# Start-up loads, stacked tails and 128-row turns in a fused attention, gated-MLP and Fourier-mixing kernel

## The chip, the core and the metric

The kernel runs on one core of a Trainium2 chip. The metric is the device time of one execution in microseconds; the median of three executions is given. One further execution was taken by the hardware profiler, and every row shown here is from it. The names in the rows: PE is TensorE's matmul stream and PEld its weight loads, DVE is VectorE, ACT is ScalarE, POOL is GpSimd, SP is SyncE; a name with a q at its end is that engine's DMA queue.

## What is computed

Attention with a soft cap on the scores, a gated MLP with a spatial projection, and a mixing layer with cosine and sine, one behind the other. Four batches, 12 heads, 448 positions, 64 numbers per head, 768 model columns.

```python
def _attn_ref(q, k, v, cap):                     # q, k, v: (4, 12, 448, 64)
    scores = np.matmul(q, k.transpose(0, 1, 3, 2)) / np.sqrt(64)
    scores = cap * np.tanh(scores / cap)
    attn = np.exp(scores - np.max(scores, axis=-1, keepdims=True))
    return np.matmul(attn / (np.sum(attn, axis=-1, keepdims=True) + 1e-09), v)

def _moe_ref(x, w_in, w_spatial, b_spatial, w_out):   # x: (4, 448, 768), w_in: (768, 1024)
    h = np.maximum(x @ w_in, 0.0)
    u, v = h[..., :512], h[..., 512:]
    v_n = (v - mean(v)) / np.sqrt(var(v) + 1e-06)
    v_s = np.einsum('ts,bsd->btd', w_spatial, v_n) + b_spatial[None, :, None]
    return (u * v_s) @ w_out

def _moe2_ref(x, w_theta, w_tok_r, w_tok_i, w_ch):
    theta = x @ w_theta
    y = einsum('ts,bsd->btd', w_tok_r, x * cos(theta)) + einsum('ts,bsd->btd', w_tok_i, x * sin(theta))
    u = x + y
    return u + np.maximum(u @ w_ch, 0.0)
```

## The kernel before

**Order of the work.** The program is written as small operations (`op(engine, due, cost, function, r=..., w=...)`) with the slots and tiles that each reads and writes. A list of numbers, `ORDER`, sorts all of them into one sequence, and every engine carries out its own part of that sequence strictly in order. An operation that waits holds back all that stands behind it on its engine, DMA issues included: loads are issued by SP, ACT or POOL in the place that the list gives them.

**Stages by time.** Heads go in pairs. The first six pairs of batch 0 are done in plain f32 ("direct"; 0 to about 80 us); the later ones as products of a high and a low part in a shorter format, with the first MLP's matmuls between them (to about 355 us). The last batch's MLP, the next layer's angles `th_ps`, the turning of `w_tok` and the mixing `y_ps` follow (to about 650 us), and then the product with `w_ch`.

**The start.** PE runs 11 matmuls on zeros (`idle`), then turns pair 0's q and k (`tqk`): rows 0 to 383 of each head from `rq` and `rk`, the last 64 rows from `tt`. Seven more `idle` matmuls follow, then the scores `sc`. A pair's scores come in groups: group 0 multiplies the last 64 keys of both heads at once, through a block-diagonal tile `bd` that DVE and ACT fill from the turned keys in PSUM. Group 1 and the others use the copy `qk`. Pair 0's loads are issued by SP and ACT, in 256-byte packets. The weights `w_in` come as 8-byte words (`w_in_bits`, 512 KB a load, 12 loads, the first six on POOL's queue) and are turned into floats by POOL (L442), DVE (L448 to L463) and POOL (L1032, L402); at most three such tiles are held at first.

**Tails of 64.** 448 positions are three blocks of 128 and one of 64. In `moe1_v` (the half of the first MLP's hidden layer that is normalised) batches 0 to 2 have their tails' high and low parts stacked as 128 columns (`beside`, tile `x_tail`). The last batch does three 64-column products instead for each of the six blocks of model columns. Turns of `w_spatial` (`w_sp_ps`) and `w_tok` (`tok_ps`) go in four matmuls against an identity each, the fourth with 64 rows.

Of the kernel before, what the change touches and what calls it, by code (L numbers as in the profile page):

```python
# [10 lines left out]
F32 = mybir.dt.float32  # L11
# [327 lines left out]
def attn_moe_moe2_kernel(ctx: ExitStack, tc: tile.TileContext, q, k, v, cap, w_in, w_sp, b_sp, w_out,  # L339
# [9 lines left out]
    SK = 4  # L349
# [147 lines left out]
    XQ = ("pool", "sp")  # L497
    HE = ("act", "act")
    LE = ("dve","dve")
    xhl = {}  # L500

    v1 = [att.tile([128, NC + 1, 2, D], F32, tag="vhl", name="v1", bufs=2) for _ in range(2)]

# [17 lines left out]
    def split_out(b, p, t):  # L521
# [4 lines left out]
        def hi():  # L526
            st["x"] = keep.tile([128, 2, S], F32R, tag="x%d" % p, name="x")
            for n, x in enumerate("hl"):
                xhl[x, b, p] = st["x"][:, n, :]
# [1804 lines left out]
```

## Time and profile before

| | |
|---|---|
| median of 3 executions | 757.33 us (756.39 to 757.44) |
| profiled execution, its own time | 756.88 us |
| its span (first to last instruction) | 755.1 us |
| PE busy | 740.6 us, 98% of the span |
| DVE, ACT, POOL busy | 601.2, 471.2, 327.6 us |

The time of an execution is that of the span plus what lies around it: here 756.88 - 755.1 = 1.8 us. Busy time is the time in which an engine had an instruction at work; what is left is idle, and a row's bracket gives the idle time just before it with the work that ended it.

### The profile page before, as it was taken

The numbers are of one execution on the slowest core, as the hardware profiler recorded it, in microseconds if no ns is written. First come the engines' busy times: TensorE is split into PE (matmuls) and PEld (weight loads), VectorE is DVE, ScalarE is ACT, GpSimd is POOL, SyncE is SP. The second block draws the span as 40 slices with busy tenths as digits, with TensorE's granted clock in tenths as the row PEclk, the third lists the DMA queues.
The fourth block names the chain that finished last, engine by engine and source line by source line (L and its number), as shares of the span: only waits on it lengthen the run. The fifth ranks groups of instructions, "written<-read, shape, count | busy, mean of one in ns | idle before, by whom it ended". The sixth has DMA issues, their size and how long they took to land.

```text
span 755.1 us, 11422 instructions
## 1 busy us (share of the span) xinstructions
PE 740.6 (98%) x3951; PEld 631.2 (84%) x3951; DVE 601.2 (80%) x979; ACT 471.2 (62%) x792; POOL 327.6 (43%) x419
## 2 busy tenths in 40 slices
PE   7999999999999999999999999999999999999997
PEld 3444678988889888988899999999989999998997
DVE  2567987888878986999987577888778887999955
ACT  2889787888788878896554545453423532554553
POOL 3537677553655465462100001332222234688570
PEclk9999999999999999999999999999999999999999
DMA  5766233242442441332243330002210000000145
GB/s 149 201 162 181 64 101 84 77 108 51 116 96 46 108 112 40 94 79 67 84 149 103 102 112 22 1 22 64 62 44 22 22 1 1 0 1 1 38 109 148
DMA packets 82718, 57.47 MB, mean 76 GB/s; under 512 B 50338, under 2 KB 75908, under 8 KB 82660
## 3 DMA queue, kind: packets, MB, share of 16 engines
q1 hardware_dynamic: 80580, 52.94, 26.9%
q0 software_dynamic: 1056, 3.54, 1.4%
q8 instruction: 31, 0.51, 0.3%
q10 hardware_dynamic: 1024, 0.26, 0.2%
q14 instruction: 27, 0.22, 0.1%
HBM read 43.72 MB, written 5.62 MB: 65 GB/s over the span
## 4 chain that ended last, share of the span: by engine, by line
PE 85%; DVE 5%; ACT 3%; DMA 3%; POOL 1%; issue 1%; SPq 0%; DVEq 0%; ACTq 0%; POOLq 0%
PE ps_mm L399 20%; PE y_ps L399 13%; PE acc L399 12%; PE th_ps L399 12%; PE f_ps L399 9%; PE sc L399 8%; PE ps_sum L399 3%; PE ps_av L399 3%; PE tqk L691 2%; PE o_ps L2155 1%; DMA w_in_bits<-in_moe_w_in_dram 1%; PE x_ps L1605 1%; ACT e L808 1%; DMA y<-y 1%; DMA rq<-in_q_dram 1%
## 5 line engine op out<-in xcount | busy, mean ns | idle before, releaser
L399 PE MATMUL y_ps<-tok_h,zt 128*128 128x448 f32 x312 | 98.5, 368 | 0.0
L805 ACT ACTIVATE e<-sc,icap 128x896 f32<-128x896 f32 x72 | 72.1, 1007 | 5.9 <-PE sc L399 5.3
L808 ACT ACTIVATE e<-e,cap_sb 128x896 f32<-128x896 f32 x72 | 74.5, 1043 | 0.6
L402 DVE TENSOR_TENSOR ll<-e,hh 128x896 fp32r<-128x896 f32 x54 | 61.2, 1136 | 8.7 <-ACT hh L813 5.6
L399 PEld LDWEIGHTS y_ps<-tok_h,zt 128*128 128x128 f32 x312 | 58.8, 188 | 4.5
L399 PE MATMUL th_ps<-th_ah,x 128*128 128x256 f32 x288 | 58.0, 285 | 0.0
L399 PE MATMUL y_ps<-tok_l,zt 128*128 128x448 f32 x156 | 57.4, 368 | 0.0
L402 POOL TENSOR_TENSOR zt<-z,zt 128x1024 fp32r<-128x1024 f32 x12 | 28.9, 2407 | 63.1 <-ACT zt L1720 63.1
L1659 POOL TENSOR_SCALAR n<-n 128x512 f32<-128x512 f32 (+1 forms) x24 | 15.8, 663 | 82.2 <-DVE n L1656 82.2
L399 PE MATMUL f_ps<-x,S 128*128 128x448 f32 x216 | 48.4, 371 | 0.3 <-POOL x L402 0.3
L399 PE MATMUL ps_mm<-x,w_in_h 128*128 128x448 f32 x168 | 48.5, 370 | 0.0
L399 PE MATMUL ps_mm<-w_in_h,x 128*128 128x512 f32 (+1 forms) x132 | 46.8, 398 | 1.2 <-DVE w_sp_l L402 1.2
L399 PEld LDWEIGHTS th_ps<-th_ah,x 128*128 128x128 f32 x288 | 47.1, 190 | 0.8
L402 POOL TENSOR_TENSOR x<-x,x 128x384 fp32r<-128x384 f32 (+1 forms) x15 | 18.5, 1239 | 66.7 <-ACT x L1546 58.4
L399 PEld LDWEIGHTS f_ps<-x,S 128*128 128x128 f32 x216 | 39.9, 188 | 3.9 <-POOL x L402 0.6
L1720 ACT CAST zt<-z 128x1024 fp32r<-128x1024 f32 (+2 forms) x36 | 24.3, 691 | 29.1 <-DVE z L1691 23.1
L895 DVE COPY s<-acc 1x448 f32<-1x448 f32 (+1 forms) x48 | 29.7, 618 | 14.0 <-ACT xun L887 6.6
L399 PE MATMUL th_ps<-th_al,x 128*128 128x256 f32 x144 | 40.7, 282 | 0.0
L399 PE MATMUL acc<-ll,vh 128*128 128x448 f32 x108 | 39.7, 368 | 0.8 <-DVE ll L402 0.8
L399 PE MATMUL acc<-hh,vh 128*128 128x448 f32 x108 | 39.6, 367 | 0.0
L399 PE MATMUL sc<-yl,XH 128*128 128x448 f32 x108 | 39.5, 366 | 0.0
L399 PE MATMUL acc<-hh,vl 128*64 128x448 f32 x108 | 39.4, 364 | 0.0
(323 smaller groups left out, 2293.9 us busy)
## 6 DMA issues: line engine op xcount, KB each, us to landing
y<-y SPq DMA_DIRECT2D x54, 112.0 KB, 2.2
bits<-in_moe_w_ch_dram SPq DMA_DIRECT2D x12, 384.0 KB, 3.1
out_dram<-o SPq DMA_DIRECT2D x23, 192.0 KB, 2.4
rq<-in_q_dram SPq DMA_DIRECT2D x33, 128.0 KB, 2.8
r<-d SPq DMA_DIRECT2D x16, 224.0 KB, 3.7
rk<-in_k_dram SPq DMA_DIRECT2D x9, 384.0 KB, 3.7
rv<-in_v_dram SPq DMA_DIRECT2D x18, 192.0 KB, 2.6
w_in_bits<-in_moe_w_in_dram POOLq DMA_DIRECT2D x6, 512.0 KB, 5.4
```

Of the source, the lines that this page charges most:

```text
L399: nc.tensor.matmul(out=ps, lhsT=a, rhs=r, start=(first and i == 0), stop=(last and i == len(terms) - 1))
L402: (engine or nc.vector).tensor_tensor(out=o, in0=x, in1=f32(hi), op=ALU.subtract)
L691: nc.tensor.transpose(o, a, ident)
L805: nc.scalar.activation(out=st["e", g], in_=src, func=ACTF.Tanh, scale=icap)
L808: nc.scalar.activation(out=st["e", g], in_=st["e", g], func=ACTF.Exp, scale=cap_sb)
L895: nc.vector.tensor_copy(out=st["s"][64 * hd:64 * hd + n, :], in_=st["acc", hd][64 - x0:64 - x0 + n, :])
L1605: nc.tensor.transpose(o, x2(b, m)[:, p * 128:p * 128 + 128], ident)
L1659: nc.gpsimd.tensor_scalar(out=sd["n"], in0=sd["n"], scalar1=1.0, scalar2=-MAGIC, op0=ALU.mult, op1=ALU.add)
L1720: nc.scalar.copy(out=o, in_=a)
L2155: nc.tensor.transpose(st["t"][0:w, i * 128:(i + 1) * 128], x2(b, m)[:, i * 128:i * 128 + w], ident)
```

## The change

It has five parts. (1) The tail of pair 0's keys is loaded through POOL's queue instead of ACT's. (2) `bd` is filled by POOL from `qk` in SBUF, for all six direct pairs, instead of by DVE and ACT from PSUM; the first `w_in` loads read the mark `begun`, which POOL's second copy of pair 0 now sets, so they stand behind it. In direct pairs group 1 is scored ahead of group 0. (3) The last batch's tails are stacked too: POOL copies them into a tile `x_tail`, which sits in the slot of the next layer's tile `x2_2` until that is opened, later than before. (4) Turns of `w_tok` and `w_spatial` take 128 rows in the fourth block, whose lower half POOL clears. (5) `ORDER` is a new list.

```diff
-            QT = ("sp", "act") if p == 0 else ("sp", "sp")
+            QT = ("sp", "pool") if p == 0 else ("sp", "sp")
...
             def block(hd):
-                copy = nc.scalar.copy if hd else nc.vector.tensor_copy
-                copy(out=bd[HD[hd], p % 2, 64 * hd:64 * hd + 64], in_=st["k"][HD[hd], 0:64])
+                nc.gpsimd.tensor_copy(out=bd[HD[hd], p % 2, 64 * hd:64 * hd + 64], in_=st["qk"][HD[hd], 1, 0:64])
-            op("act", t0 - FR - 5.2, ca, lambda: plain(0), r=ks, w=[kqk] + ["begun"] * (b == p == 0), banks=ks[:1])
+            op("act", t0 - FR - 5.2, ca, lambda: plain(0), r=ks, w=[kqk], banks=ks[:1])
...
-                op(("dve", "act")[hd], t0 - FR - 4.9, 0.2, lambda hd=hd: block(hd), r=ks, w=[(kb, hd)], banks=ks[1:])
+                op("pool", t0 - FR - 4.2, 0.25, lambda hd=hd: block(hd), r=[kqk, (kqk, 1)],
+                   w=[(kb, hd)] + ["begun"] * (b == p == hd - 1 == 0), port=True)
...
+        if direct:
+            steps[:2] = [(1, 0.0, 4, 0.8, 2.3, 3.25, 3.8), (0, 1.4, 3, 1.9, 3.2, 3.85, 4.15)]
...
+            if j == 3:
+                nc.gpsimd.memset(st["p"][UP, 3, :], 0.0)
...
-                nc.tensor.transpose(st[i][0:m, j * 128:j * 128 + n], st["p"][0:n, j, i * 128:i * 128 + m],
-                                    ident[0:n, 0:n])
+                nc.tensor.transpose(st[i][0:m, j * 128:j * 128 + 128], st["p"][:, j, i * 128:i * 128 + m], ident)
...
-        beside = i == SK - 1 and b < B - 1
+        beside = i == SK - 1
+        kx = "xt" if b < B - 1 else "xu"
+        if beside and b == B - 1:
+            def tail(j):
+                if "x" not in x_last:
+                    x_last["x"] = pools["xs"].tile([128, NP, 2, 64], F32R, tag="x2_%d" % (B - 2), name="x_tail")
+                x = f32(xpair[b, j])
+                nc.gpsimd.tensor_scalar(out=x_last["x"][:, j], in0=x[:, :, 384:448], scalar1=1.0, scalar2=0.0,
+                                        op0=ALU.mult, op1=ALU.add)
...
-                        products(ps, [(xt_[:, j].rearrange("p a n -> p (a n)"), wi["h", 1, j])], first, last)
+                        x = xt_ if b < B - 1 else x_last["x"]
+                        products(ps, [(x[:, j].rearrange("p a n -> p (a n)"), wi["h", 1, j])], first, last)
...
+        def pad():
+            ta[1] = gpool.tile([128, 2, 2 * S], F32, tag="g", name="ta")
+            nc.gpsimd.memset(ta[1][UP, 1, :], 0.0)
...
-                a, o = ta[j // 2][0:n, j % 2], st["ps"][:, j * 128:j * 128 + n]
+                a, o = ta[j // 2][:, j % 2], st["ps"][:, j * 128:j * 128 + 128]
                 if kk < NC:
-                    nc.tensor.transpose(o, a[:, kk * 128:(kk + 1) * 128], ident[0:n, 0:n])
+                    nc.tensor.transpose(o, a[:, kk * 128:(kk + 1) * 128], ident)
...
+    op("none", u - 1.0, 0.0, lambda: open_x2(B - 2), w=[("x2", B - 2, m) for m in range(KD)] + ["x_last"]
+       + [("xu" + x, j) for x in "hl" for j in range(KD)])
```

Three places show how instructions move. The first is POOL's list from the first instruction behind the start barrier; `v_103` and `v_104` are two tiles of values whose columns of ones and zeros POOL sets. Before:

```order
masks.py:197 MEMSET ident 128x128
L1019 DMA w_in_bits<-in_moe_w_in_dram 128x512
masks.py:199 ISA
masks.py:199 AFFINE_SELECT ident<-ident 128x128
L1019 DMA w_in_bits<-in_moe_w_in_dram 128x512
L505 MEMSET v_103 128x3x64
L506 MEMSET v_103 128x3x64
L507 MEMSET v_103 128x256
L508 MEMSET v_103 64x64
L509 MEMSET v_103 64x64
L442 TENSOR_SCALAR w_in_bits<-w_in_bits 128x512 x2
L1019 DMA w_in_bits<-in_moe_w_in_dram 128x512
```

The same place in the changed kernel:

```order
L511 MEMSET v_103 64x64
L512 MEMSET v_103 64x64
L615 DMA tt<-in_k_dram 64x2x64
L748 COPY bd<-qk 64x64 x2
L1026 DMA w_in_bits<-in_moe_w_in_dram 128x512 x2
L508 MEMSET v_104 128x3x64
L509 MEMSET v_104 128x3x64
L510 MEMSET v_104 128x256
L511 MEMSET v_104 64x64
L512 MEMSET v_104 64x64
L1026 DMA w_in_bits<-in_moe_w_in_dram 128x512
L748 COPY bd<-qk 64x64
```

Ahead of these rows the changed list has only the identity and the other `v_103` settings, so the first two `w_in` loads, which were the second and the fifth row, now stand behind the load of the keys' tail and behind two copies that need pair 0's turned keys.

The second place is PE's list in the last batch's `moe1_v`, at the first of its 64-column products; `ps_sum` belongs to the other half of the hidden layer. Before:

```order
L399 MATMUL ps_mm<-w_in_h,x 64x512
L399 MATMUL ps_mm<-w_in_l,x 64x512
L399 MATMUL ps_mm<-w_in_h,x 64x512 x2
L399 MATMUL ps_mm<-w_in_l,x 64x512
L399 MATMUL ps_mm<-w_in_h,x 64x512 x2
L399 MATMUL ps_mm<-w_in_l,x 64x512
L399 MATMUL ps_mm<-w_in_h,x 64x512
L399 MATMUL ps_sum<-w_in_h,x 128x512
```

The same place in the changed kernel:

```order
L400 MATMUL ps_mm<-w_in_h,x_tail 128x512
L400 MATMUL ps_mm<-w_in_l,x 64x512 x2
L400 MATMUL ps_mm<-w_in_h,x_tail 128x512
L400 MATMUL ps_mm<-w_in_l,x 64x512
L400 MATMUL ps_mm<-w_in_h,x_tail 128x512
L400 MATMUL ps_mm<-w_in_l,x 64x512
L400 MATMUL ps_mm<-w_in_h,x_tail 128x512
L400 MATMUL ps_mm<-w_in_l,x 64x512
L400 MATMUL ps_mm<-w_in_h,x_tail 128x512
L400 MATMUL ps_sum<-w_in_h,x 128x512
```

For each block of model columns two 64-column products with `w_in_h` became one with 128 columns; over the whole tail 18 matmuls became 12.

The third place is PE's list at the first turn of `w_tok`, between two products of the angles. Before:

```order
L399 MATMUL th_ps<-th_ah,x 128x256
L1481 MATMUL tok_ps<-ident,ta 128x128 x3
L1481 MATMUL tok_ps<-ident,ta 128x64
L1481 MATMUL tok_ps<-ident,ta 128x128 x3
L1481 MATMUL tok_ps<-ident,ta 128x64
L399 MATMUL th_ps<-th_ah,x 128x256
```

The same place in the changed kernel:

```order
L400 MATMUL th_ps<-th_ah,x 128x256
L1509 MATMUL tok_ps<-ident,ta 128x128 x8
L400 MATMUL th_ps<-th_ah,x 128x256
```

Each turn of 64 rows became one of 128, in the same place; there are nine such among the turns of `w_tok` and four among those of `w_spatial`.

## Rows read from the trace of the kernel before

**Rows 1.** The page: its span and the engines' busy time.
```profile
span 755.1 us, 11422 instructions
PE 740.6 (98%) x3951; PEld 631.2 (84%) x3951; DVE 601.2 (80%) x979; ACT 471.2 (62%) x792; POOL 327.6 (43%) x419
```

**Rows 2.** Windows: stretch, length, busy us of each engine, granted clock, DMA share, GB/s.
```profile
20.00:60.00 40.00, 40.00 (x145) 17.00 (x144) 24.93 (x42) 34.21 (x50) 20.14 (x23) 1.00 0.69 190
60.00:70.00 10.00, 9.63 (x33) 3.78 (x33) 5.63 (x10) 9.93 (x15) 7.17 (x10) 1.00 0.64 164
80.00:90.00 10.00, 8.32 (x39) 6.21 (x38) 9.88 (x13) 7.45 (x11) 3.99 (x6) 1.00 0.13 39
90.00:100.00 10.00, 9.17 (x45) 6.98 (x44) 9.14 (x9) 7.76 (x12) 6.81 (x9) 1.00 0.34 82
350.00:450.00 100.00, 100.00 (x488) 89.77 (x487) 80.95 (x160) 51.62 (x105) 8.70 (x11) 1.00 0.35 105
```

**Rows 3.** Timeline of PE, 0 to 20 us: start, us, engine, line, operation, [idle before].
```profile
1.18 4.88 PE L515 MATMUL idle<-zero 128*128 128x512 bf16 x11 [1.18 <-DVE zero L374]
9.75 0.87 PE L677 MATMUL tqk<-ident,rq 128*128 128x128 f32 x3 [3.70 <-DMA tt<-in_k_dram]
11.55 2.82 PE L515 MATMUL idle<-zero 128*128 128x512 bf16 x7
16.00 0.55 PE L677 MATMUL tqk<-ident,rq 128*128 128x128 f32 x3
19.30 1.02 PE L399 MATMUL sc<-qk,bd 128*128 128x448 f32 x2 [0.35 <-ACT e L805]
```

**Rows 4.** Timeline of SP and POOL, the start: issues, a setting, the first conversion.
```profile
1.29 0.74 POOL L1019 DMA_DIRECT2D w_in_bits<-in_moe_w_in_dram  x1 [0.36 <-issue]
1.55 1.45 SPq L601 DMA_DIRECT2D rq<-in_q_dram  x2
3.36 0.33 POOL L507 MEMSET v<- 128x256 f32 x1
7.20 0.64 POOL L442 TENSOR_SCALAR w_in_bits<-w_in_bits 128x512 f32<-128x512 f32 x1 [3.10 <-DMA w_in_bits<-in_moe_w_in_dram]
```

**Rows 5.** DMA packets by queue, 3.0 to 4.5 us, then 8.0 to 9.0 us.
```profile
q0 software_dynamic: 87, 0.34, 80.7%
q10 hardware_dynamic: 45, 0.01, 3.4%
...
q1 hardware_dynamic: 1004, 0.23, 113.8%
```

**Rows 6.** Timeline of DVE and POOL: first conversion of `w_in`, its fourth load, `w_sp_p`.
```profile
17.42 0.41 DVE L448 TENSOR_SCALAR w_in_f<-w_in_bits 128x512 uint32<-128x512 uint32 x1
20.54 0.58 POOL L1019 DMA_DIRECT2D w_in_bits<-in_moe_w_in_dram  x1
69.48 2.76 POOL L1070 TENSOR_SCALAR w_sp_p<-w_sp_n 128x384 f32<-128x384 f32 x6
```

**Rows 7.** Timeline of PE: turns of `w_spatial`, the last batch's tail, turns of `w_tok`, of `x`.
```profile
72.60 1.43 PE L1077 MATMUL w_sp_ps<-ident,w_sp_p 128*128 128x128 f32 x8
73.96 1.77 PE L399 MATMUL acc<-e,v 128*128 128x448 f32 x4
...
363.92 0.39 PE L399 MATMUL ps_mm<-w_in_l,x 128*64 128x512 f32 x1
364.15 0.61 PE L399 MATMUL ps_mm<-w_in_h,x 128*64 128x512 f32 x2
...
454.18 1.37 PE L1481 MATMUL tok_ps<-ident,ta 128*128 128x128 f32 x8
455.49 0.38 PE L399 MATMUL th_ps<-th_ah,x 128*128 128x256 f32 x1
...
466.96 0.82 PE L1605 MATMUL x_ps<-ident,x 128*128 128x128 f32 x6
467.62 0.27 PE L1607 MATMUL x_ps<-ident,x 128*128 128x128 f32 x1
```

More of the change, by code (lines that the diff above doesn't have):

```diff
@@ L500, in attn_moe_moe2_kernel @@
     xhl = {}
+    xpair = {}
+    x_last = {}
     v1 = [att.tile([128, NC + 1, 2, D], F32, tag="vhl", name="v1", bufs=2) for _ in range(2)]
@@ L529, in hi @@
                 xhl[x, b, p] = st["x"][:, n, :]
+            xpair[b, p] = st["x"]
             if HE[b > 0] == "act":
@@ L909, in attention @@
         K = {}
-        for g, ts, n, tt, te, th, tl in ((0, 0.0, 3, 0.65, 2.3, 2.95, 3.25), (1, 0.6, 4, 1.4, 2.9, 3.85, 4.4),
-                                         (2, 2.6, 4, 3.8, 4.7, 5.95, 6.5), (3, 4.8, 4, 5.7, 6.6, 7.8, 8.7)):
+        steps = [(0, 0.0, 3, 0.65, 2.3, 2.95, 3.25), (1, 0.6, 4, 1.4, 2.9, 3.85, 4.4),
+                 (2, 2.6, 4, 3.8, 4.7, 5.95, 6.5), (3, 4.8, 4, 5.7, 6.6, 7.8, 8.7)]
+        if direct:
+            steps[:2] = [(1, 0.0, 4, 0.8, 2.3, 3.25, 3.8), (0, 1.4, 3, 1.9, 3.2, 3.85, 4.15)]
+        for g, ts, n, tt, te, th, tl in steps:
             ks = ring("s", 2)
@@ L1075, in transposes @@
             for j in range(SK):
-                n = 128 if j < 3 else 64
-                nc.tensor.transpose(st[i][0:m, j * 128:j * 128 + n], st["p"][0:n, j, i * 128:i * 128 + m],
-                                    ident[0:n, 0:n])
+                nc.tensor.transpose(st[i][0:m, j * 128:j * 128 + 128], st["p"][:, j, i * 128:i * 128 + m], ident)
         def hi(i):
@@ L1154, in relu @@
             nc.scalar.activation(out=st["v"], in_=st["ps"][0:n, 0:HF], func=ACTF.Relu)
-        beside = i == SK - 1 and b < B - 1
+        beside = i == SK - 1
[7 more added lines that the diff above has]
+                                        op0=ALU.mult, op1=ALU.add)
+            for j in range(KD):
+                op("pool", due - 4.0 + 0.3 * j, 0.3, lambda j=j: tail(j), r=[("xh", j), ("xl", j), "region"],
+                   w=[("xuh", j), ("xul", j)] + (["x_last"] if j == 0 else []), port=True)
         def step(j, ps, first, last):
@@ L1193, in moe1_v @@
             (0.43 if beside else 0.65, j,
-             [("w", x, 1, j) for x in "hl"] + [("xh", j), ("xl", j)] + [("xt" + x, j) for x in "hl"] * beside)
+             [("w", x, 1, j) for x in "hl"] + [("xh", j), ("xl", j)] + [(kx + x, j) for x in "hl"] * beside)
             for j in range(KD)], span, early, lambda ps, j, first, last: step(j, ps, first, last))
@@ L1298, in close_attention @@
             wo[x] = pools["w15"].tile([128, KF, DM], F32R, name="w_out_" + x)
-        for b in range(B - 1):
-            x2_tiles[b] = pools["xs"].tile([128, KD, S], F32, name="x2_%d" % b)
+        for b in range(B - 2):
+            open_x2(b)
     p15 = ExitStack()
@@ L1304, in attn_moe_moe2_kernel, with open_x2 @@
     x2_tiles = {}
+    def open_x2(b):
+        x2_tiles[b] = pools["xs"].tile([128, KD, S], F32, name="x2_%d" % b)
     def x2(b, m):
@@ L1432, in load_tok @@
         slots = [ring("g", 3), ring("g", 3)]
+        def pad():
+            ta[1] = gpool.tile([128, 2, 2 * S], F32, tag="g", name="ta")
+            nc.gpsimd.memset(ta[1][UP, 1, :], 0.0)
+        op("pool", t - 1.0, 0.5, pad, r=["region"], w=[slots[1]])
         for j in range(SK):
@@ L1477, in transposes @@
             for j in range(SK):
-                n = 128 if j < 3 else 64
-                a, o = ta[j // 2][0:n, j % 2], st["ps"][:, j * 128:j * 128 + n]
+                a, o = ta[j // 2][:, j % 2], st["ps"][:, j * 128:j * 128 + 128]
                 if kk < NC:
-                    nc.tensor.transpose(o, a[:, kk * 128:(kk + 1) * 128], ident[0:n, 0:n])
+                    nc.tensor.transpose(o, a[:, kk * 128:(kk + 1) * 128], ident)
                     continue
-                nc.tensor.transpose(o, a[:, S - 128:S], ident[0:n, 0:n])
-                nc.tensor.transpose(o[LO], a[:, S:S + 64], ident[0:n, 0:n])
+                nc.tensor.transpose(o, a[:, S - 128:S], ident)
+                nc.tensor.transpose(o[LO], a[:, S:S + 64], ident)
         def dst(x):
```

335 rows, old and new, of the table ORDER are left out of this document.

## The prediction

> **What bounds the kernel now.** I read the page first: PE is busy 740.6 of 755.1 us [rows 1], so nothing can gain much unless it shortens PE's work or fills one of its 14.5 us of pauses. The windows show where these are. The last batch's MLP has none, PE 100.00 of 100 us [rows 2]. From 80 to 100 us PE has 8.32 and 9.17 of 10, and there DVE has 9.88 and 9.14: 2.5 us of pauses in a stretch that DVE sets, with an ACT at 9.93 of 10 just ahead of it (60 to 70). PE's timeline of the first 20 us shows the largest pause: its zero matmuls end at 6.06, its first turn starts at 9.75 [rows 3]. That is 3.7 us, a quarter of all.
>
> **The start.** The bracket of that pause names a load of key tails, but the instruction waits on the two loads of pair 0's queries (issued 1.55, [rows 4]) and on the identity. SP has issued both by 1.55 + 1.45 = 3.0 us; what is late is the data. POOL issues `w_in` at 1.29, and in 3.0 to 4.5 us its queue q0 holds 80.7% of the DMA time with 87 packets, while q1, the queries' queue, has no row at all and q10, ACT's, moves 45 packets [rows 5]. With `w_in` nearly gone, q1 moves 1004 packets in the one microsecond from 8.0. Pair 0's q and k are 1792 packets (four loads of 384 and two of 128): at that rate 1.8 us. If they flow from 3.0 us, when SP has issued both query loads, they are there at 4.8 us, and with a few hundred packets of pair 1 mixed in at 5.3. The key tail goes through POOL behind five settings of at most 0.33 us each [rows 4] and the identity; I estimate its issue at 2.7 us and the landing of its 128 packets under 6. All that is before the zero matmuls end at 6.06. So the first turn moves from 9.75 to about 6.1: **3.6 us**. If packets still get in each other's way by a microsecond, 2.7.
>
> A rule weighed against that: the Trainium skill, DMA: Bandwidth & Descriptors, Queues, rings and completion order, says that each DMA engine goes round the queues that have work, a packet at a time. By that rule the queries should have had every second turn beside `w_in`, and the loads would be slow by themselves. The row with no q1 packet does not agree. By the rule the start would gain a microsecond instead of 3.6, which is rival B.
>
> **The clock in the start.** The granted clock reads 1.00 in every stretch, but spacings say more: eleven 512-column zeros take 4.88 us, so about 0.43 each, which is the lower level (1.2 GHz); late in the kernel 512 columns take 0.23 (363.92 to 364.15, [rows 7]). Three turns take 0.87 us at 9.75 and 0.55 at 16.00 [rows 3]. So PE reached its upper level only after the turns, having worked on without a break from 9.75. In the changed kernel it works on from 1.18 with no pause at 6.06. If the upper level comes as late behind the turns as now, nothing is gained; if it is there when the turns begin, the seven zeros take 7 x 0.23 = 1.6 instead of 2.8 us and the six large turns 2 x 0.32 less: 1.8 us. I take **1.2**, nearer the upper end, since by 6.1 us PE will have worked unbroken longer than it had before the present rise; the earlier 4.88 us did not raise it, so I don't take all.
>
> **What now stands behind POOL's copies.** `bd` needs DVE's `qk` copy first and then two POOL copies; group 1 goes first, so PE asks for `bd` only after one group of scores and pair 1's turns, over 2 us later. Hidden. ACT loses its six copies, and with group 1 first the 0.35 us pause at 19.30 should go: **0.35** (0 to 0.35).
>
> The first `w_in` load moves from 1.29 to about 9.5 us. Before, it landed for POOL at 7.20 and DVE touched it at 17.42 [rows 4, 6]: ten microseconds to spare. Landing some 5.9 us after its issue, as now, gives 15.4, where DVE, moved up by 4.8 to 5.2 us with PE, would want it at about 12.4. The chain starts 3 us late against PE. The fourth load waits for a freed tile (20.54), not for the first load; DVE is busy only 24.93 of 40 us from 20 to 60 [rows 2], so I let the chain catch up, at nothing. If it does not, see rival C.
>
> **Stacked tail.** The 64-column products have the spacing of whole ones, 0.23 us (363.92 to 364.15), [rows 7]; 18 become 12: 6 x 0.23 = **1.4 us** on a PE without pauses. POOL's six copies lie beside (POOL 8.70 of 100 us there, [rows 2]), as do the three added operations of ACT and DVE.
>
> A rule that speaks against it: the Trainium skill, TensorEngine Tiling (Array Packing), Tiling Modes, has 128-by-64 tiles that work independently of each other. By it, pairs of 64-column products side by side would cost half, and stacking would gain nothing, which is rival E. The spacing shows no such overlap here: by the row the term is 1.4, by the rule 0.
>
> **Turns by 128 rows.** Eight turns with two of 64 rows take 454.18 to 455.49 = 1.31 us; turns of 128 rows alone have a spacing of 0.66 / 6 = 0.11 (466.96 to 467.62), [rows 7]. Eight of them, the last followed closely, take about 0.80. So 0.26 us per 64-row turn: three blocks of eight give 1.5, the block of four 0.26, the last block, with its two at the end, 0.2. Sum **2.0 us**, PE having no pause there. POOL's clearing of the padding lies long before.
>
> For `w_spatial` the first block of eight takes 72.60 to 73.96, 1.36 us, so 0.5 could be saved there and 0.55 in the other two. But all of it lies ahead of or inside the stretch that DVE sets, and DVE's list there is the same: **0** (at most 1.05).
>
> **Sum.** 3.6 + 1.2 + 0.35 + 1.4 + 2.0 = 8.55 us. The profiled execution took 756.88, so 748.3; it lies 0.45 below the median of the three, so I give **748.5 us**. The forecast's own range: starts of 2.7 to 3.7, clock 0 to 1.8, pauses 0 to 0.35, tail 1.4, turns 1.9 to 2.1, `w_spatial` 0 to 1.05: 6.0 to 10.4 gained, or 746.7 to 751.1.
>
> **Rivals.**
>
> B. The queries are slow by themselves: their 256-byte packets, not `w_in`, set the 9.75. For it: q10's packets come slowly too, and with 8.0 to 9.0 us full the rate is bound by packets. Against it: the empty q1. The start then gains about 1 and the clock nothing: 1.0 + 0.35 + 1.4 + 2.0 = 4.75, so 752.6.
>
> C. The start's gain is lost again at 60 to 100 us. ACT and then DVE set the pace there, and what feeds them is also the `w_in` chain. If that stays 3 us late against PE, then PE pauses longer before its turns of `w_spatial`, whose source `w_sp_p` POOL finishes at 69.48 + 2.76 = 72.24 [rows 6], 0.36 before PE takes it. Of its 3 us some 0.4 are PE's to spare there, and 2.6 of the 8.55 go: 751.1.
>
> D. Slower. The whole `w_in` chain hangs on its first load and moves with it. That load lands at 15.4 instead of 7.2, 8.2 us later; `w_sp_p` would be done at 80.4, where PE arrives at 72.6 - 5.15 = 67.4: a stall of 13 us, against gains of 8.55, so 757.3 + 4.4 = 761.7. It decides from the point at which the chain is late by more than the 8.55 gained plus the 0.36 to spare, less the 5.15 that PE comes early: 3.8 us later than now at 72 us. Against it: the ten microseconds for which the first tile lay unused, and a fourth load that waits for the conversion.
>
> E. The 64-column products lie side by side already, and stacking gains nothing: 748.5 + 1.4 = 749.9. Against it: their spacing of 0.23 us, that of whole ones.
>
> **Chances.** Forecast 0.68, B 0.11, C 0.11, D 0.04, E 0.03, other mishaps 0.03. A measurement of this kernel tells 0.2%, 1.5 us, from no change. Faster by more than that are the forecast, B, C and E: 0.93; the same 0.03; slower 0.04. The range takes in B's and C's times and the forecast's lower end: 746.3 to 752.6.
>
> **What would show it.** PE's first turn at about 6.1 and no pause ahead of it; first scores at about 9.5; zeros between them under 2.8 us; `w_in` issues behind the `bd` copies, at 9 to 10; no q0 rows before them but the tail's; no pause of PE that POOL's `bd` ends; 12 matmuls in the last batch's tail at 0.23; blocks of eight turns at 0.8. The prediction is wrong if the first turn starts after 7, if PE's pauses from 80 to 100 us grow by more than 1 us over 2.5, or if waits for `x_tail` or `x2_2` appear where PE had none.

## The result, and the profile after

The changed kernel takes **749.46 us** (median of 4 executions, 748.24 to 750.56); the kernel before, beside it on the same chip, 756.86 us (756.06 to 757.44). The ratio is 0.9903, with a 95% interval of 0.9881 to 0.9924: 7.4 us, or 1.0%, faster. 748.5 us was forecast. The profiled execution took 750.56 us, one of the slower two of the four; a second profile of the same kernel took 748.49 (it is the run `after_again` below).

The page of the changed kernel, its span and busy times, answers to [rows 1]:

```profile
span 748.8 us, 11416 instructions
PE 735.2 (98%) x3945; PEld 629.0 (84%) x3945; DVE 606.3 (81%) x974; ACT 471.6 (63%) x787; POOL 335.1 (45%) x440
```

PE's work fell by 5.4 us and its pauses from 14.5 to 13.6. With the start's pause of 3.7 filled, 10.8 should have been left: so 2.8 us more of them came elsewhere than went. The windows of the changed kernel, beside [rows 2], show where:

```profile
20.00:60.00 40.00, 39.83 (x148) 16.97 (x147) 29.62 (x40) 35.49 (x50) 25.62 (x33) 1.00 0.76 202
70.00:80.00 10.00, 7.74 (x34) 5.12 (x33) 9.80 (x15) 7.61 (x15) 5.97 (x11) 1.00 0.26 72
80.00:90.00 10.00, 9.16 (x44) 7.00 (x43) 9.20 (x9) 7.01 (x10) 5.49 (x7) 1.00 0.33 88
90.00:100.00 10.00, 10.00 (x47) 7.95 (x46) 7.89 (x12) 7.31 (x11) 7.34 (x12) 1.00 0.52 135
350.00:450.00 100.00, 99.64 (x494) 89.55 (x493) 81.03 (x162) 51.61 (x105) 11.59 (x18) 1.00 0.34 105
```

The program stands some 6 us further on in the same window, so the stretch that DVE fills now lies at 70 to 80 us, and PE has 2.3 us of pauses in it. What was not there before is in the last row: PE pauses by 0.36 us in the last batch's MLP, where it had none.

PE's timeline from 0 to 20 us, beside [rows 3]:

```profile
1.18 4.87 PE L518 MATMUL idle<-zero 128*128 128x512 bf16 x11 [1.18 <-DVE zero L375]
5.85 0.85 PE L681 MATMUL tqk<-ident,rq 128*128 128x128 f32 x3
7.22 1.67 PE L518 MATMUL idle<-zero 128*128 128x512 bf16 x7
8.82 1.02 PE L400 MATMUL sc<-qk 64*128 64x448 f32 x4
18.45 0.92 PE L400 MATMUL sc<-qk,bd 128*128 128x448 f32 x2
```

The first turn starts at 5.85 without a bracket: there is no pause ahead of it. The seven zeros take 1.67 us in place of 2.82, and the first score starts at 8.82. In the kernel before that was at 14.20:

```profile
14.20 0.92 PE L399 MATMUL sc<-qk,bd 128*128 128x448 f32 x2
```

No product that needs `bd` has a bracket. The timeline of SP, POOL and DVE in the same stretch, beside [rows 4, 6]:

```profile
0.73 1.58 SPq L605 DMA_DIRECT2D rq<-in_q_dram  x2
...
2.25 0.80 POOL L615 DMA_DIRECT2D tt<-in_k_dram  x1
8.12 0.50 POOL L748 COPY bd<-qk 64x64 f32<-64x64 f32 x2 [5.06 <-DVE qk L745]
8.56 1.15 POOL L1026 DMA_DIRECT2D w_in_bits<-in_moe_w_in_dram  x2
...
13.11 0.43 DVE L449 TENSOR_SCALAR w_in_f<-w_in_bits 128x512 uint32<-128x512 uint32 x1 [1.44 <-DMA w_in_bits<-in_moe_w_in_dram]
```

SP issues the two loads of pair 0's queries at 0.73, in [rows 4] at 1.55: the new list moved them too. `w_in` is issued at 8.56, behind the two copies into `bd`, and DVE now waits 1.44 us for it; in [rows 6] it had lain ready for ten. The DMA packets by queue from 3.0 to 4.5 us, the window of [rows 5]:

```profile
q1 hardware_dynamic: 576, 0.14, 41.5%
q10 hardware_dynamic: 361, 0.09, 26.2%
q0 software_dynamic: 29, 0.03, 6.8%
```

q1, which had no packet there, moves 576. PE's timeline at the last batch's tail and at the first turn of `w_tok`, beside [rows 7]:

```profile
365.13 0.40 PE L400 MATMUL ps_mm<-w_in_h,x_tail 128*128 128x512 f32 x1
365.88 0.48 PE L400 MATMUL ps_sum<-gh,w_out_h 128*128 128x448 f32 x1 [0.36 <-ACT vt L1161]
...
449.81 1.03 PE L1509 MATMUL tok_ps<-ident,ta 128*128 128x128 f32 x8
450.60 0.36 PE L400 MATMUL th_ps<-th_ah,x 128*128 128x256 f32 x1
```

Eight turns take 0.79 us (449.81 to 450.60) in place of 1.31. At the end of the stacked tail PE waits for ACT, where the kernel before went on.

### The profile page after: what moved, and what is told of

Read it like the earlier page. It is cut to its first block, busy times and chain, and to the rows that moved or that the text cites. A ratio compares the mean times of both kernels' runs of the same rounds, so it can differ in the third digit from the quotient of the medians.

```text
span 748.8 us, 11416 instructions
## 1 busy us (share of the span) xinstructions
PE 735.2 (98%) x3945; PEld 629.0 (84%) x3945; DVE 606.3 (81%) x974; ACT 471.6 (63%) x787; POOL 335.1 (45%) x440
## 4 chain that ended last, share of the span: by engine, by line
PE 78%; DVE 13%; ACT 3%; POOL 2%; issue 2%; DMA 1%; SPq 0%; DVEq 0%; ACTq 0%; POOLq 0%
PE ps_mm L400 17%; PE y_ps L400 12%; PE th_ps L400 11%; PE acc L400 10%; PE f_ps L400 8%; PE sc L400 8%; PE ps_sum L400 3%; PE ps_av L400 3%; PE tqk L695 2%; DVE x L403 1%; PE o_ps L2185 1%; DVE ll L403 1%; DVE s L983 1%; PE x_ps L1635 1%; DVE xun L986 1%
## 5 line engine op out<-in xcount | busy, mean ns | idle before, releaser
L403 POOL TENSOR_TENSOR zt<-z,zt 128x1024 fp32r<-128x1024 f32 x12 | 30.4, 2533 | 66.8 <-ACT zt L1750 66.8
L400 PE MATMUL ps_mm<-w_in_h,x 128*128 128x512 f32 x120 | 43.1, 398 | 3.1 <-DVE w_sp_l L403 1.7
L1707 ACT ACTIVATE z<-z 128x512 f32<-128x512 f32 (+1 forms) x24 | 12.5, 523 | 41.6 <-DVE z L1701 41.4
```

What stands on the lines that cost most here:

```text
L400: nc.tensor.matmul(out=ps, lhsT=a, rhs=r, start=(first and i == 0), stop=(last and i == len(terms) - 1))
L403: (engine or nc.vector).tensor_tensor(out=o, in0=x, in1=f32(hi), op=ALU.subtract)
L1707: nc.scalar.activation(out=z[:, 0:n_], in_=r[:, 0:n_], func=ACTF.Sin)
```

## The experiments

Each was run with executions of the kernel before on the same chip, and the ratio is to those. "a" in a name is the changed kernel with an edit, "b" the kernel before with one.

| run | median, us | ratio to before, 95% interval |
|---|---|---|
| the changed kernel | 749.46 | 0.9903 [0.9881, 0.9924] |
| after_again | 749.38 | 0.9892 [0.9876, 0.9908] |
| a_win_first | 755.92 | 0.9976 [0.9961, 0.9991] |
| a_zeros5 | 751.58 | 0.9927 [0.9908, 0.9946] |
| b_start | 755.80 | 0.9980 [0.9966, 0.9993] |
| b_parts | 754.59 | 0.9958 [0.9941, 0.9975] |
| b_fix | 753.42 | 0.9953 [0.9934, 0.9971] |
| a_tok64 | 751.53 | 0.9928 [0.9914, 0.9942] |
| a_sp64 | 749.72 | 0.9896 [0.9881, 0.9911] |
| a_tail64 | 750.18 | 0.9902 [0.9888, 0.9916] |
| a_cast | 751.07 | 0.9914 [0.9896, 0.9932] |
| a_order | 748.51 | 0.9880 [0.9859, 0.9900] |
| a_both | 747.24 | 0.9869 [0.9851, 0.9888] |

Differences of a microsecond between medians are within what executions of one kernel differ by; for such the profiles are set side by side, from one landmark in the program to the next.

### The changed kernel a second time

> The changed kernel once more, for a second profile. Its four executions so far lie in two pairs, 748.2 and 748.6, 750.3 and 750.6, and the profile at hand is of the upper pair. Theory: the upper pair is made by a load of reciprocals (r<-d) that lands late at 318.8 us, after which VectorE works without a gap to 345 us and TensorE pauses 0.92 and 1.37 us; then a profile of a lower execution shows that load landing 1 us or more sooner and less than 1 us of these two pauses. Rival: the upper pair has the clock's upper level later in the start; then the first score stands after 9.5 us in one pair and at 8.8 in the other. Time expected: 749.4, from 748 to 751.

749.38 us; its span is 746.7, 2.1 shorter than that of the profile above. The first score is at 8.93, so the start is not what differs. The pauses differ: at 74, 77, 319 and 505 us the slower execution has 0.4 to 0.6 us more each. The theory holds for one of its two pauses: that at 319 goes from 0.92 to 0.37, that at 342 is 1.37 in both. Where two profiles are compared below, this one stands for the changed kernel.

### The start: whose loads come first

The first two `w_in` loads go back to the head of POOL's list:

```diff
+for i in (44, 30):
+    ORDER.remove(i)
+    ORDER.insert(0, i)
...
-        op("pool" if pool else "sp", t - 9.0, 1.05 if pool else 0.53, load, w=[kb], r=["begun"], lag=4.0, early=0.0)
+        op("pool" if pool else "sp", t - 9.0, 1.05 if pool else 0.53, load, w=[kb], r=["begun"] * (half == 0 or kk not in (0, 2)), lag=4.0, early=0.0)
```

> The changed kernel with the first two loads of w_in back at the head of GpSimd's list; nothing else differs. Theory (the loads of w_in hold the 256-byte packets back): the first turn goes from 5.85 back to 9 to 10 us, the upper clock level comes only after the turns, the first score stands at 13 to 14.3 instead of 8.8 us, and the time rises by 4 to 5.5 us to 753.5 to 755. Rival (the new order of the q and k loads, queries first, is what helped): first turn at 5.9 to 7, time within 1.5 us of 749.5.

755.92 us, 6.5 more than the changed kernel and a microsecond over the upper end of the expectation. PE's timeline of this run, up to 14 us:

```profile
1.18 4.16 PE L522 MATMUL idle<-zero 128*128 128x512 bf16 x11 [1.18 <-DVE zero L379]
6.87 0.52 PE L685 MATMUL tqk<-ident,rq 128*128 128x128 f32 x3 [1.52 <-DMA rq<-in_q_dram]
8.81 0.37 PE L687 MATMUL tqk<-ident,tt 64*128 64x64 f32 x1 [1.43 <-DMA tt<-in_q_dram]
10.36 3.19 PE L522 MATMUL idle<-zero 128*128 128x512 bf16 x7
13.48 1.12 PE L404 MATMUL sc<-qk 64*128 64x448 f32 x2
```

With `w_in` ahead the queries' loads are late again (two pauses, 2.95 us), the zeros between are back at 3.19 us for seven, and the first score comes 4.6 us later. The order of the issues on POOL does this: all other edits of the start are still in. The other 1.9 us are behind the first score, where profiles of the changed list differ by as much (337.4 to 340.0 us from the first score to the last `acc`, 339.3 here). The first turn, at 6.87 and not at 9 to 10, is earlier than the theory had it: with SP's query loads issued at 0.73 the first two come sooner, as the rival has it, but the turns of the tails then wait.

### The clock: zeros left out

```diff
-    warm_up(11, -9.0, [])
+    warm_up(5, -9.0, [])
```

Six of the first matmuls on zeros are left out; the output does not depend on them.

> The changed kernel (749.4, first turn 5.85, first score 8.8 us) with 5 zero matmuls ahead of the first turn instead of 11, so TensorE pauses from 3.3 us until the loads have landed. It shows when they land: theory, between 5.0 and 5.85 us. Theory of the clock (the upper level came at 6.3 us because TensorE had worked without a break from 1.2): with the break the turns and most of the seven zeros behind them run at the lower level, first score at 9.5 to 11 us, time 0.7 to 2 us up. Rival (the level comes at its own time, break or not): first score at 8.2 to 8.9 us, time within 0.6 us of 749.4.

751.58 us, 2.2 longer. PE's timeline of this run:

```profile
5.03 0.88 PE L681 MATMUL tqk<-ident,rq 128*128 128x128 f32 x3 [1.54 <-DMA rq<-in_q_dram]
6.83 3.19 PE L518 MATMUL idle<-zero 128*128 128x512 bf16 x7
9.95 1.73 PE L400 MATMUL sc<-qk 64*128 64x448 f32 x4
```

This run shows two things. The queries are there at 5.03 us, so the changed kernel's first turn, at 5.85, comes 0.8 us later than they allow. And PE, which paused for 1.54 us, turns 0.8 earlier but runs its seven zeros in 3.19 / 7 = 0.46 us each (the lower level, 1.2 GHz) where the changed kernel, with no pause, runs them in 1.67 / 7 = 0.24 (the upper, 2.4 GHz); the four scores take 1.73 us, not 1.02. At the first score the changed list with all zeros is ahead by 1.0 us (8.93 in `after_again`); the rest of the 2.2 comes later, where profiles of one list differ by as much. The granted clock reads 1.00 in these stretches all the same.

`a_zeros5` has both a pause and fewer matmuls. `a_win_first`, with all eleven zeros, tells them apart: its eleven take 4.16 us in place of 4.87, since the last are spaced 0.22 (the upper level), the three turns at 6.87 take 0.52, and behind the second pause the seven zeros take 3.19. Here the granted clock shows the fall too; its window from 9 to 12 us, with the clock third from the end:

```profile
9.00:12.00 3.00, 2.81 (x9) 1.42 (x9) 0.94 (x3) 0.53 (x1) 0.61 (x3) 0.50 0.59 106
```

The column has 0.95 from 7 to 8 us and 0.50 from 8 to 9: the level that PE had reached was lost in the second pause. Work without a break from 1.18 us gives the upper level before the seven zeros, and that is worth more than turning 0.8 us earlier.

### What the new order list is for

First the start alone (parts 1 and 2 of the change) on the kernel before, with the old list; then all parts of the code with the old list, in which the operations that are new were put in by hand. The renumbered lists are left out of the cut.

```diff
-            QT = ("sp", "act") if p == 0 else ("sp", "sp")
+            QT = ("sp", "pool") if p == 0 else ("sp", "sp")
...
+                op("pool", t0 - FR - 4.2, 0.25, lambda hd=hd: block(hd), r=[kqk, (kqk, 1)],
+                   w=[(kb, hd)] + ["begun"] * (b == p == hd - 1 == 0), port=True)
...
+            steps[:2] = [(1, 0.0, 4, 0.8, 2.3, 3.25, 3.8), (0, 1.4, 3, 1.9, 3.2, 3.85, 4.15)]
```

> The kernel before with the start's part alone: the key tail on GpSimd's queue, bd copied by GpSimd from qk, group 1 ahead of group 0, the first w_in loads behind the second copy; its old order otherwise, no stacked tail, turns of 64 rows. Theory (the start's gain comes through to the end, 3.7 of pause and some 1.7 of clock): first score near 8.9 us, time 5 us under the kernel before, 751 to 752.8. Rival (the stretch that VectorE sets, 75 to 100 us, or w_in's chain swallows it): pauses from 70 to 100 us grow from 2.5 to 4 us or more and the time is 753.5 or above.

> All code parts of the change (start, stacked tail, turns of 128 rows) in the old order, new instructions put in by hand. Theory (the parts give the gain and the new list costs 1 to 2 us by new pauses from 240 to 510 us): 5.2 + 1.4 + 2.0 + 0 to 1 = 8.6 to 9.6 us under the kernel before, 747.3 to 748.3, so faster than the changed kernel. Rival (the new list is needed to make the parts pay): slower than the changed kernel, 750.5 or above, with new pauses behind the moved instructions.

`b_start` gains 1.5 us by its ratio, though its first score comes at 8.97, as early as in the changed kernel. At the first turn of the seventh pair it is 3.3 us ahead of the kernel before (67.58 against 70.90), where the changed kernel is 7.0 ahead (63.95 in `after_again`): 3.7 us of new pauses lie between. From 70 to 100 us its pauses are the 2.5 us of the kernel before. The timeline of DVE and PE in `b_start` shows the first place:

```profile
13.20 0.43 DVE L434 TENSOR_SCALAR w_in_f<-w_in_bits 128x512 uint32<-128x512 uint32 x1 [5.00 <-DMA w_in_bits<-in_moe_w_in_dram]
14.78 0.62 DVE L727 COPY qk<-tqk 128x448 f32<-128x448 f32 x1
...
15.54 0.99 PE L385 MATMUL sc<-qk 64*128 64x448 f32 x3 [1.88 <-ACT et L794]
```

DVE stands on the first `w_in` load, which now comes late, until 13.20, and pair 1's copy into `qk` stands behind that step in DVE's list. Its input, PE's turns of pair 1, is there by 11.96 (11.41 + 0.55). PE needs the copy and waits 1.88 us; the bracket names ACT's `et`, which ended last by the profile, but the copy ends at 15.40. At 57 us the same comes again on ACT: it waits 1.77 us for a later `w_in` load, two copies out of the accumulator stand behind it, and PE pauses by 1.37 and 0.43. `b_parts`, with everything in the code, is at 754.59, as its rival has it and not its theory: it has these pauses too (2.01 us at 12.6, 1.19 and 0.82 at 56 and 59). Between it and the changed kernel lies only the list: about **5 us** by the medians, 4.3 by the spans of the two profiles (751.0 and 746.7). How much of it hangs on where the new operations were put by hand was not tried.

To test that reading, three entries of `b_start`'s list are moved: DVE's steps on `w_in` behind pair 1's copy, and ACT's scaling behind the two copies.

```diff
+for i, behind in ((33, 27), (32, 27), (101, 222)):
+    ORDER.remove(i)
+    ORDER.insert(ORDER.index(behind) + 1, i)
```

> The kernel before with the change of the start alone, in the old order (755.8 us), and three entries of that order moved: on DVE the copy of pair 1's q and k goes ahead of the two first steps of the conversion of w_in, and on ACT one scaling of w_in's bits (at 56.9 us) goes behind two copies out of the accumulator. Theory: the start gains 5.2 us at the first score, and the old order gives it back because in-order engines stand on a w_in load that comes late (PE pauses of 1.88, 1.37 and 0.43 us). Then these three moves bring 2 to 3.5 us: 752.3 to 753.8, with no pause at 13.7 and none over 0.5 at 57 to 60. Rival: the old order loses time everywhere, PE being early against all that was planned around it; then pauses only move, and the time stays at 755 to 756.

753.42 us, 2.4 less than `b_start` (2.0 by the ratios), within what the theory gave. By the profiles the moves make less of it: from an equal first score (8.97) `b_fix` is ahead by 1.5 us at the first `acc`, 1.2 at the first `ps_mm` and 1.0 at the last `acc`; another 1.2 us is a pause at 550 us, far from what was moved, that its profile lacks. Its timeline of DVE and PE:

```profile
11.99 0.62 DVE L731 COPY qk<-tqk 128x448 f32<-128x448 f32 x1 [3.80 <-PE tqk L672]
14.02 1.02 PE L389 MATMUL sc<-qk 64*128 64x448 f32 x4 [0.36 <-ACT e L795]
...
57.79 0.43 DVE L438 TENSOR_SCALAR w_in_f<-w_in_bits 128x512 uint32<-128x512 uint32 x1 [2.31 <-POOL w_in_l L392]
58.93 0.62 DVE L731 COPY qk<-tqk 128x448 f32<-128x448 f32 x1
59.70 1.02 PE L389 MATMUL sc<-qk 64*128 64x448 f32 x4 [2.33 <-ACT x L521]
```

The first pause is cured (1.88 to 0.36). At 57 us ACT no longer holds PE up, but PE pauses by 2.33, not by 1.37 and 0.43: one step on, DVE stands on the `w_in` chain (2.31 us) with the last pair's copy behind it. So both theories had a part: the cause is the one named, and it sits at more places than three entries reach. The new list has none of these pauses.

### The three parts with less or other work for PE

Each part is taken back alone. Turns of `w_tok`, and in another kernel those of `w_spatial`, by 64 rows in the fourth block again:

```diff
-                a, o = ta[j // 2][:, j % 2], st["ps"][:, j * 128:j * 128 + 128]
+                n = 128 if j < 3 else 64
+                a, o = ta[j // 2][0:n, j % 2], st["ps"][:, j * 128:j * 128 + n]
...
-                nc.tensor.transpose(st[i][0:m, j * 128:j * 128 + 128], st["p"][:, j, i * 128:i * 128 + m], ident)
+                nc.tensor.transpose(st[i][0:m, j * 128:j * 128 + n], st["p"][0:n, j, i * 128:i * 128 + m],
+                                    ident[0:n, 0:n])
```

> The changed kernel (749.4) with the turns of w_tok by 64 rows in the fourth block again, all else the same. Theory (each 64-row turn costs 0.26 us more, on a TensorE without pauses): blocks of eight at 1.3 instead of 0.8 us, the last y_ps 2.0 us later than in the second profile of the changed kernel (658.9 to 659.1 instead of 657.0), time 2.0 us up at 751.4. Rival (the gain is given back by pauses behind the turns): the last y_ps within 0.7 us of 657.0, time within 0.7 us of 749.4.

> The changed kernel (749.4) with the turns of w_spatial by 64 rows in the fourth block again. The prediction's step: what is saved here is taken back by the stretch that VectorE sets, so the first product ps_mm stands within 0.3 us of the 77.9 us of the second profile, and the time within 0.5 us of 749.4. Rival (TensorE paces this stretch too): ps_mm 0.7 to 1.1 us later, time 0.7 to 1.1 us up.

`a_tok64` is at 751.53 us. Between the first and the last turn of `w_tok` its profile falls behind that of `after_again` by 2.01 us, and by 0.34 in the 448 us ahead of them: the part is worth 2.0. `a_sp64` is at 749.72. At its last turn of `w_spatial` it is 0.60 later than at its first, measured against `after_again`; at the first product behind the turns, which waits for DVE, it is 0.06 earlier. PE's pause there is 0.48 in place of 1.31 us. From the first turn to that product it takes 12.2 us, kernels with 128-row turns and the changed list 12.2 to 13.4, so no gain can be told. What PE saves in these turns it waits for DVE.

The last batch's tail in 64-column products again:

```diff
-            if beside:
+            if beside and b < B - 1:
...
-            nc.scalar.copy(out=st["t"][UP], in_=st["ps"][UP, 0:HF])
+            if b < B - 1:
+                nc.scalar.copy(out=st["t"][UP], in_=st["ps"][UP, 0:HF])
+            else:
+                nc.scalar.activation(out=st["v"], in_=st["ps"][0:n, 0:HF], func=ACTF.Relu)
...
```

POOL's copies into `x_tail` and the two steps behind the eviction are left out as well.

> The changed kernel (749.4) with the last batch's tail in 64-column products again: 18 matmuls, no copies into x_tail, one eviction instead of three. Theory (64-column products have the spacing of whole ones): the first turn of w_tok 1.4 us later than the 448.2 us of the second profile, time 1.4 us up at 750.8. Rival (such products lie side by side): within 0.4 us of 448.2 and of 749.4. Third way: the pauses of 0.36 at 363.9 us, which the kernel before does not have, belong to the stacked tail's evictions; then 1.0 instead of 1.4.

750.18 us, ratio 0.9902. Against `after_again` its profile is 1.80 us behind ahead of the tail (last `acc`, 348.16 against 346.36) and 1.86 behind it (last `ps_mm`, 445.10 against 443.24): six matmuls fewer, 1.4 us of PE, bring 0.06. That stretch is steady: six profiles with the stacked tail and the changed list take 96.86 to 96.88 us for it. The timeline of ACT and PE in `a_tail64`:

```profile
365.16 0.60 ACT L1161 ACTIVATE vt<-ps_sum 128x512 f32<-128x512 f32 x1 [0.98 <-DVE vn_l L403]
...
366.67 0.39 PE L400 MATMUL ps_mm<-w_in_h,x 128*64 128x512 f32 x1
366.90 0.36 PE L400 MATMUL ps_sum<-gh,w_out_h 128*128 128x448 f32 x1
```

ACT copies block 2 out of `ps_sum` at 365.16, held up by DVE's `vn_l` of the block ahead. PE reaches `ps_sum` at 366.90 and finds it free. In the changed kernel ACT comes at 365.23, also behind `vn_l`, and PE, which entered the stretch at nearly the same time (last `acc` 347.95), is there at 365.13 + 0.23 = 365.36, 1.5 us sooner: it waits until 365.88, and then again for DVE's `w_out_l` and `gl` (in `after_again` five spacings of 0.25 to 0.47 us at 365.8 to 368.7, in place of 0.21). `a_tail64` has no spacing over 0.26 us from the last `acc` to the last `ps_mm`, and is 0.06 us longer. What ACT and DVE do there takes about as long as PE's work with 18 products, so six fewer bring nothing.

DVE is busy for 15.5 of 16 us from 352 to 368 us in `after_again`, so the next run takes 1.3 us of work from it:

```diff
-        op("dve", t + 3.2, 0.34, lambda: nc.vector.tensor_copy(out=vn["h"][0:n, i, :], in_=st["v"]), r=[kv],
+        hi = "act" if b == B - 1 and i < SK - 1 else "dve"
+        op(hi, t + 3.2, 0.34, lambda: (nc.scalar.copy if hi == "act" else nc.vector.tensor_copy)(
...
```

> The changed kernel with three copies taken from DVE to ACT: the rounding of the last batch's normalized v of blocks 0 to 2 (0.43 us each on DVE). Theory: between 352 and 368 us DVE, busy for 15.5 of 16, sets the pace, and that is why six products fewer bring nothing there; with 1.3 us less on DVE the spacings of PE at 363.5 to 368 go back toward 0.21 us, and 0.6 to 1.2 us come: 748.2 to 748.8. Rival: the stretch hangs on the loads of w_out or on ACT's in-order work, not on DVE's throughput; then 749.4 or, with ACT later, up to 750.

751.07 us: the gain that the theory gave does not come. The waits of `a_cast` from 356 to 372 us (us in total, times, longest):

```profile
DVE vn_l L403 <- ACT vn_h L1231: 1.4, 2, 0.7
PE ps_sum L400 <- ACT vt L1161: 0.7, 1, 0.7
```

DVE has less to do and stands idle for it: it waits twice for the copies that are now ACT's, and PE's pause at `ps_sum` grows from 0.36 to 0.74 us. From last `acc` to last `ps_mm` the kernel loses 0.47. So work that goes from DVE to ACT does not shorten this stretch, since DVE waits for it there. The rows fit a chain that goes to and fro between ACT and DVE and grows with each crossing. That is not shown: the edit adds crossings as well as taking work away, ACT also waits for loads of `w_out` there (0.9 us each), and which link would have to be shorter was not tried.

### Mending the new list

The changed kernel has pauses that the old one had not, at 247 and 342 us. The one at 77 (1.74 in the profile above, 1.31 in `after_again`) is not new, though the expectation below counts it so: the kernel before has one ahead of the same product, 1.19 us up to 86.24. The timeline of DVE, POOL and PE at 342:

```profile
339.81 1.08 DVE L403 TENSOR_TENSOR ll<-e,hh 128x896 fp32r<-128x896 f32 x1
340.81 1.88 DVE L986 TENSOR_TENSOR xun<-xun,r 128x448 f32<-128x448 f32 x1
342.73 0.62 DVE L1257 TENSOR_TENSOR gated<-gated,ps_mm 128x448 f32<-128x448 f32 x1
...
339.98 1.34 POOL L836 TENSOR_SCALAR et_hl<-et 64x448 fp32r<-64x448 f32 x1 [2.44 <-DVE xun L986]
341.29 0.93 POOL L821 TENSOR_SCALAR hh<-e 128x896 fp32r<-128x896 f32 x1
...
343.40 0.50 PE L400 MATMUL ps_mm<-w_in_h,x 128*128 128x512 f32 x1 [1.37 <-DVE gated L1257]
```

PE waits for DVE's product into `gated`, whose input has been ready since 340.3; ahead of it in DVE's list stands a product `xun` that is needed later and takes 1.88 us. Three entries are moved, one at each of the three pauses:

```diff
+for i, before in ((1620, 1500), (1135, 1111)):
+    ORDER.remove(i)
+    ORDER.insert(ORDER.index(before), i)
+ORDER.remove(232)
+ORDER.insert(ORDER.index(318) + 1, 232)
```

> The changed kernel with three entries of its order list moved, each at a pause that the old kernel did not have: DVE's w_spatial rest ahead of an x rest (75.3 us), ACT's tanh ahead of a copy out of the accumulator (245.7), DVE's product into gated ahead of a normalizing product (339.2). Theory: the pauses of 1.31, 0.61 and 1.37 us are made by the order alone, so most of 3.3 us comes back: 746.5 to 747.5. Rival: DVE and ACT are full there, and what is moved back is missed next; then 749 to 750, with pauses a microsecond or two later.

> The edits of the two kernels before together (three casts on ACT, three entries of the order moved). If both theories hold, their gains add, since the stretches lie apart: 745.5 to 747. If neither does, 749.4.

748.51 and 747.24 us. In `a_order` the pause at the `gated` product is gone and so is that at 247; of the one at 77 (1.31 in `after_again`) 0.69 is left, at the next `w_sp_l`. DVE's timeline of `a_order` at the `gated` product:

```profile
338.53 0.62 DVE L1263 TENSOR_TENSOR gated<-gated,ps_mm 128x448 f32<-128x448 f32 x1
339.07 1.23 DVE L992 TENSOR_TENSOR xun<-xun,r 128x448 f32<-128x448 f32 x1
```

At the last `acc` it is 1.91 us ahead of `after_again`. By the medians the gain is 0.9, with executions from 746.03 to 750.20, so the ratio's interval overlaps that of the changed kernel; that the pauses went is shown, the gain in time is not told from none by the medians. `a_both` has the best median, 2.1 us under that of `after_again`, and its intervals overlap too. The profiles say more: from the first score to the last `acc` `a_order` takes 336.3 us and `a_both` 335.3, seven profiles with the changed list 337.4 to 340.0. From there to the last `ps_mm` `a_order` loses 0.42 us against `after_again`, `a_cast` 0.47 and `a_both` 0.94, so the losses add. What is left of the lead of `a_both`, 1.69 us of 2.63, was made ahead of the tail, where only the list differs.

## Why the prediction was right, step by step

**The start's pause, 3.6.** First turn 9.75 to 5.85: 3.9 us, as forecast from the packets of q1. The queries landed at 5.03, as `a_zeros5` shows, between the 4.8 and 5.3 that were worked out. That it fits so well is partly luck: I let the packets flow from 3.0, but the new list has SP issue both loads by 2.31 (0.73 + 1.58), so they took 2.7 us from there and not 1.8. That the earlier issue is not what fills the pause, `b_start` shows: there SP issues them at 1.55 as before, and the first turn is at 5.84 without a pause. Rival B, that the queries are slow by themselves, falls with `a_win_first`: the same loads are late when `w_in` is ahead and not when it is behind. By the rule of the Trainium skill (DMA: Bandwidth & Descriptors, Queues, rings and completion order) the queues are served by turns; the kernel before does not agree, with no packet of q1 from 3.0 to 4.5 us beside 87 of q0. The 576 packets with `w_in` behind say only that the queries are quick alone.

**The clock, 1.2.** The first score came 5.38 us earlier (14.20 to 8.82), 1.48 more than the first turn. Of that 1.05 lie between the first of the seven zeros and the first score (2.65 before, 1.60 now), 0.43 in the turns ahead. The reason held, that work without a pause brings the upper level sooner, and so did not taking all of 1.8: the first three turns still take 0.85 us. The size is partly luck, since the level does not come at one point: in `b_parts` the last of the eleven zeros are already spaced 0.22, in the changed kernel none. In the eleven profiles with `w_in` behind and eleven zeros the first score lies between 7.93 and 8.97.

**`bd` and the pause at 19.30, 0.35.** No product with `bd` waits; the pause is gone.

**The late `w_in` chain, nothing.** This step is right for the changed kernel and was right for the wrong reason. I let the chain catch up because DVE was not full. In `b_start` it does not: an engine that has time stands on the late load all the same, with what PE needs queued behind it, and 3.7 of 5.2 us go. That is rival C's mechanism at another place, in the lists of DVE and ACT at 13 and 57 us instead of at `w_sp_p` on POOL. What hid the chain is part 5 of the change, the new list, to which I gave no term. It is worth 4 to 5 us beside the other four parts.

**The stacked tail, 1.4.** This is the term that was mis-sized: 0.06. I read "no pause in 100 us" as "PE sets the pace". PE and the chain through ACT and DVE were nearly level; with 1.4 us taken from PE the chain showed, as the pause at 365.88. DVE's 80.95 of 100 us in [rows 2] hid that it was busy for 14.45 of the 15 us from 353 to 368, which should have made me look for such a chain. The window of the kernel before (PE, PEld, DVE and so on):

```profile
353.00:368.00 15.00, 15.00 (x67) 11.59 (x67) 14.45 (x26) 5.98 (x12) 2.11 (x4) 1.00 0.18 54
```

Which link of that chain sets it stays open. Rival E gave the same nothing for another reason, 64-column products side by side (a rule of the Trainium skill's TensorEngine Tiling (Array Packing), Tiling Modes); in `a_tail64` they are 0.23 us apart, as in [rows 7], so that reason is not borne out.

**`w_tok` 2.0, `w_spatial` nothing.** Both as measured: 2.01, and nothing that can be told (-0.06).

**What the sum did not have.** The spans of the three profiles, cut at landmarks of PE, in us:

| stretch | before | profile above | after_again |
|---|---|---|---|
| to the first score | 14.20 | 8.82 | 8.93 |
| to the seventh pair's first turn | 56.70 | 55.29 | 55.02 |
| to the first `ps_mm` | 15.34 | 15.02 | 13.99 |
| to the last `ps_mm` | 363.67 | 365.68 | 365.30 |
| to the last turn of `w_tok` | 30.81 | 28.86 | 28.86 |
| to the end | 274.38 | 275.13 | 274.60 |

The second row gains 1.4 to 1.7, of which two pauses that are gone make 0.59 (0.35 ahead of 19.30, 0.24 at 63.6); the rest I did not take apart. It does not seem to be the list's: in `b_start`, with the old one, the stretch takes 58.6 us with 3.7 of new pauses, so 54.9 without them. The fourth row loses 1.6 to 2.0: the new list's pauses at 247, 319 and 342 us make 2.9 us there in the profile above, where the old list had 0.84 (at 297 and 325). Neither had a term. They nearly cancel. The start's 0.6 too little makes up for a part of the tail's 1.3 too much. The third row, up to the first product behind the turns of `w_spatial`, gains 0.3 in one profile and 1.35 in the other. The start and `w_tok` were right by their mechanism; that the total came out so close is luck: 8.55 forecast, 7.4 and 8.1 measured by the medians.

None of the three signs of being wrong came: the first turn is at 5.85, the pauses from 70 to 100 us, where the stretch that DVE sets now lies, are 3.1 us and 2.1 in `after_again`, against 2.5, and for `x_tail` or `x2_2` PE waits nowhere (from 366 to 505 us it has no pause). One bound of the prediction does not come out of its terms: they give 746.7 as the forecast's lower end, and the range has 746.3.

## What to carry to other kernels

A load that is moved behind more urgent ones must have its consumers moved too: on engines that work in order, the step that waits for it holds up everything behind it, however idle the engine. An engine without a pause is not proof that it sets the pace; before counting a saving on it, look at what its neighbours' chain has to spare in that same stretch, in windows as short as the stretch. Where a change brings a new order along, run the new code in the old order too: here that gave 3 of the 7.4 us, and showed that the rest hung on the list.

## What was not expected of the hardware

A DVE operation with two inputs in SBUF can be stretched by what POOL does. `xun<-xun,r` takes 0.61 to 0.63 us in 10 of its 16 places, but 1.88 at 340.81 above and 2.41 at 75.59, each time with POOL at work beside it. In three such cases (two of this profile, one of `after_again`) DVE's row ends 0.47 to 0.49 us after POOL's last, and so it does in the kernel before (2.41 at 82.71). Not every overlap stretches DVE: at 249.79 the row takes 0.56 wholly beside 1.07 us of POOL's `et_hl`. The timeline of DVE and POOL in the changed kernel at 75.59:

```profile
75.59 2.41 DVE L986 TENSOR_TENSOR xun<-xun,r 128x448 f32<-128x448 f32 x1
...
75.44 0.75 POOL L550 DMA_DIRECT2D x_tail<-x  x1 [0.83 <-DVE x L403]
76.22 1.30 POOL L403 TENSOR_TENSOR vl<-rv,vh 128x512 fp32r<-128x512 f32 x1
```

The Trainium skill, SBUF — State Buffer, Who interferes with whom, has a rule for it: a DVE instruction with two SBUF inputs contends with a GpSimd instruction that reads SBUF. The stretched rows agree. No run here took POOL's work away to test it. The two stretches add 1.8 and 1.3 us to DVE, and pauses of PE of 1.74 and 1.37 follow them, at 77 and 342 us; that the stretches make them is not shown. The pause at 342 is gone in `a_order`, where `xun` still takes 1.23 but stands behind the `gated` product.

The granted clock reads 1.00 from the first window on, while the same matmul on zeros takes 0.44 us at 1.18 and 0.24 at 7.22. In the first 9 us here the level is read from spacings, not from that column; a later fall stands in it, as the 0.50 in `a_win_first` shows.
